# Low halves on VectorE alone, and the denominator's first step on ScalarE, in a top-k attention, expert and rational-layer kernel

## The chip, the cores and the metric

The kernel runs on one core of one Trainium2 chip. The metric is device microseconds (us) of one execution; the kernel before took 1326.49 us, the median of three runs (1324.46 to 1328.33). The engines are TensorE (PE in the profile, its weight loads PEld), VectorE (DVE), ScalarE (ACT), GpSimd (POOL) and SyncE (SP, which issues most DMAs).

## The reference, cut to what matters

```python
# 1. attention, 4 x 8 heads, 576 positions, head size 64, only the 32 largest scores of a row kept
# 2. routing: of all (token, expert) pairs, best first, each of 2304 tokens gets one of 8 experts,
#    each expert takes 288 tokens; then h = relu(x @ w1[e]) ; x2 = h @ w2[e]      (512 -> 1024 -> 512)
# 3. one more layer for all tokens, with a rational function in the middle:
h = x2 @ w_in                                    # 512 -> 2048
P = a[0] + a[1] * h + a[2] * h2 + a[3] * h3
Q = 1.0 + abs(b[0]) * abs(h) + abs(b[1]) * h2
out = (P / (Q + 1e-6)) @ w_out                   # 2048 -> 512
```

## The kernel before, in words

**Three stages.** First the attention, in 72 steps of 128 rows. Then the routing: seven phases, each of which finds by a search of four iterations the score down to which tokens are handed out (`route`, `search`, lines 1520 to 1735). An iteration is a chain: VectorE compares all tokens with 32 thresholds (L1502), TensorE counts (L1510), VectorE looks which thresholds are passed (L1574), TensorE spreads that (L1578), VectorE makes the next thresholds (L1586). At the end of a phase GpSimd marks the tokens handed out (L1665). Then the experts, one after the other, 288 tokens each: the first two products on `w1[e]` and `w2[e]` (the experts' own weights, made ready one expert ahead), and 16 units of the rational layer, each a slice of 128 of the 2048 columns.

**Matrices in two halves.** A float32 matrix is scaled by a power of two and stored as a high half and a low half in 16 bits; a product is then three 16-bit matmuls (`triple`, L1902 to L1904). ScalarE makes the high half (`high`, L437), and a second operation takes scaled value minus high half for the low one. `w_in` and `w_out` are cut in 32 pieces of 128 x 512, in four blocks of four each (`add_block`). A piece arrives by DMA, passes through some operations that rebuild its bits (`heads` on ScalarE, L374 to L386, and `mantissa`, `signed`, `apply_sign` on VectorE, L396 to L413), its sum of squares is taken (L307), the block gets its scale, and high and low halves follow. The high halves of a block wait for the low halves of the block before (L476), and the low half's end frees the raw piece's buffer; if a piece is still to come that may lie there, its DMA is issued then (`fetch`). Pieces 0 to 17 have buffers at the start; 18 to 23 wait for low halves; 24 to 31 lie where the first expert's raw weights were. The scales of all blocks of `w_out` together (`settle_out`) enter the rational layer's result, before its second product.

**A planner writes the order.** Each operation is a task with an engine, a cost, dependencies and a rank. `Flow.run` emits the task with the earliest start by its own reckoning, by rank where these tie; each engine then executes its instructions in the order written. During the search VectorE's tasks are emitted by `fill`, which is given a budget of 0.6 or 0.37 us at each place (J1, J2, J3 in L1529) and lets a VectorE task in only if its whole cost fits. Tasks of other engines only have to be able to start in time. After the search `flow.early` and, for the units, `flow.rest` emit all that is left. A low half is a VectorE task of cost 0.66 (L441) with an alternative: two GpSimd operations, cost 2.3, L449 and L450. The planner takes the alternative where GpSimd could start no later than 1 us after VectorE.

**A unit** (`add_unit`, from line 2151): TensorE makes `ph` (12 matmuls). ScalarE: z = |h| (L2169), uv = a3 h + a2 (L2172). VectorE: q = b1 z + b0 (L2175), q times z (L2178), uv times h (L2181), cube3 (L2193), which is the last to read `ph`. ScalarE: logarithm and exponential, for 1/Q (L2184, L2187). VectorE: two steps of correction (L2190, L2196) and the ratio (L2199). ScalarE and VectorE make its two halves (L1892, L1893), and TensorE adds 12 matmuls into `po`. `ph` has two buffers.

Of the kernel before, what the change touches and what calls it, by code (L numbers as in the profile page):

```python
# [8 lines left out]
F32 = mybir.dt.float32  # L9
# [5 lines left out]
AF = mybir.ActivationFunctionType  # L15
OP = mybir.AluOpType
# [168 lines left out]
def kernel(  # L185
# [15 lines left out]
    nc = tc.nc  # L201
# [5 lines left out]
    P = 128  # L207
# [40 lines left out]
    coef = consts.tile([P, 16], F32, name="coef")  # L248
# [81 lines left out]
    raw_t, todo = {}, list(range(NP - 8))  # L330

    flow = Flow()
# [3 lines left out]
    def fetch(slot, n=None):  # L336

        if n is None and todo and todo[0] <= slot[1]:
            n = todo.pop(0)
        if n is not None:  # L340
            nc.sync.dma_start(slot[0].bitcast(U16)[:, 0:2047], pieces[n][:, 1:2048])
            raw_t[n] = slot
            arrived[n].end = flow.transfer(1.5)
        elif slot[2] is not None:
            slot[2]()

    def value(n):
        return raw_t[n][0].rearrange("p (n w) -> p n w", w=2)[:, :, 1]
# [7 lines left out]
    def quick(n):  # L356
        return QS <= n < QE
# [36 lines left out]
    def signed(n, o):  # L394
        up = upper_of(n)[:, o]
        nc.vector.scalar_tensor_tensor(up, top_of(n)[:, o], 0x8000, up, op0=OP.bitwise_and, op1=OP.bitwise_or)  # L396

    def in_parts(cost, fn, deps, rank, late, hv=None):

        w = 512 // (hv or HV)  # L400
        return [
            flow.add("V", 0.06 + (cost - 0.06) * w / 512, lambda o=o: fn(slice(o, o + w)), deps, rank, late)
            for o in range(0, 512, w)
        ]
# [6 lines left out]
    def apply_sign(n, o=ALL):  # L411
        d = value(n).bitcast(F32)[:, o]
        nc.vector.tensor_tensor(d, d, sign(n)[:, o], op=OP.mult)  # L413
# [6 lines left out]
    def add_block(i, n0, dst, s, inv, rows, rank, late, after):  # L420

        o = slice(4 * i, 4 * i + 4) if rows else slice(i, i + 1)
        sq = wpool.tile([P, 4], F32, name="nq", bufs=8)
        steps = []
        n2 = sq
        if not rows:
            n2 = wpool.tile([P, 1], F32, name="nq1", bufs=8)
            steps.append(("V", 0.07, lambda: nc.vector.tensor_reduce(n2, sq, axis=AX.X, op=OP.add)))
        steps += [("V", 0.07, f) for f in power_steps(s[:, o], inv[:, o], n2, 410)]

        def part(g):
            j = 4 * i + g if rows else i
            return j, [d[:, j, :] if rows else d[:, i, g * 512 : (g + 1) * 512] for d in dst]

        def high(g):
            j, (h, l) = part(g)
            nc.scalar.activation(h, value(n0 + g).bitcast(F32), AF.Copy, scale=s[:, j : j + 1])  # L437

        def low(g):
            j, (h, l) = part(g)  # L440
            nc.vector.scalar_tensor_tensor(  # L441
                l, value(n0 + g).bitcast(F32), s[:, j : j + 1], h, op0=OP.mult, op1=OP.subtract
            )
            fetch(raw_t.pop(n0 + g))

        def low_pool(g):
            j, (h, l) = part(g)
            d = value(n0 + g).bitcast(F32)
            nc.gpsimd.tensor_tensor(d, d, s[:, j : j + 1].to_broadcast([P, 512]), op=OP.mult)  # L449
            nc.gpsimd.tensor_tensor(l, d, h, op=OP.subtract)  # L450
            fetch(raw_t.pop(n0 + g))

        norms = []
        for g in range(4):
            n = n0 + g
            t = [arrived[n]]
            if quick(n):
                first = flow.add("A", 0.52, lambda n=n: heads(n)[0][2](), t, rank + 0.5, late)
                t = flow.add("A", 0.52, lambda n=n: heads(n)[1][2](), [first], rank + 0.5, late)
                t = in_parts(0.6, lambda o, n=n: signed(n, o), [t], rank + 0.4, late)  # L460
                t = in_parts(0.6, lambda o, n=n: mantissa(n, o), t, rank + 0.3, late)
                take(first, ring_users, ZR, t)
            else:
                for k in range(3 if n >= 6 else 0):
                    t = [flow.add("A", (0.52, 0.52, 0.61)[k], lambda n=n, k=k: heads(n)[k][2](), t, rank + 0.5, late)]
                if n >= EV:
                    t = in_parts(0.6, lambda o, n=n: mantissa(n, o), t, rank + 0.4, late)
                    t = in_parts(0.6, lambda o, n=n: apply_sign(n, o), t, rank + 0.3, late)
            norms.append(
                flow.add("A", 0.61, lambda n=n, g=g: square(value(n).bitcast(F32), sq[:, g : g + 1]), t, rank + 0.2, late)  # L470
            )
        scaled = flow.chain(steps[:-1], norms, rank, late)
        lows, LOWS = [], after
        last = flow.chain(steps[-1:], [scaled], rank + 0.3, late)
        for g in range(4):
            t = flow.add("A", 0.61, lambda g=g: high(g), [scaled] + (lasts[-1] if lasts else []), rank + LOWS, late)  # L476
            t = flow.add("V", 0.66, lambda g=g: low(g), [t], rank + LOWS + 0.1, late)
            t.other = ("G", 2.3, lambda g=g: low_pool(g))
            lows.append(t)
        lasts.append(lows)  # L480
        return last
# [1383 lines left out]
    mp = ctx.enter_context(tc.tile_pool(name="mp", bufs=1, side="right"))  # L1865
# [8 lines left out]
    xe_t, tok_t, xT_t, hT_t, x2_t, sq_t, py_t, scl, bt = {}, {}, {}, {}, {}, {}, {}, {}, {}  # L1874
# [163 lines left out]
    def unscale(e):  # L2038
        inv2 = mp.tile([P, 1], F32, name="inv2", bufs=2)
        nc.vector.tensor_scalar(inv2, w_scale[1, e][1], w_scale[2, e][1], k_h, op0=OP.mult, op1=OP.mult)  # L2040
        inv2a = mp.tile([P, 1], F32, name="inv2a", bufs=2)
        nc.vector.tensor_scalar(inv2a, inv2, coef[:, 3:4], None, op0=OP.mult)
        back = mp.tile([P, 2], F32, name="back", bufs=2)
        nc.vector.tensor_scalar(
            back[:, 0:1].bitcast(I32), inv2.bitcast(I32), -1.0, float(254 << 23), op0=OP.mult, op1=OP.add
        )
        nc.vector.tensor_scalar(back[:, 1:2], back[:, 0:1], coef[:, 0:1], None, op0=OP.mult)
        scl[e] = [inv2, None, None, inv2a, back[:, 1:2]]

    def bound_steps(e):  # L2050
        st = {}
# [51 lines left out]
    for t in range(NT):  # L2103
        nc.gpsimd.memset(spacer, 0.0)
        s = nc.gpsimd.indirect_dma_start(
            out=order, out_offset=bass.IndirectOffsetOnAxis(ap=sloti[:, t : t + 1], axis=0),
            in_=row_id[:, t : t + 1], in_offset=None,
        )
# [42 lines left out]
    def add_unit(k):  # L2151

        e, f = divmod(k, NF2)
        st = {}
# [9 lines left out]
        def tile(name, n):  # L2164
            st[name] = tp.tile([P, CAP], F32, name=name, bufs=n)
            return st[name]
# [2 lines left out]
            nc.scalar.activation(tile("z", 3), st["ph"], AF.Abs, scale=scl[e][0])  # L2169

        def cube():
            nc.scalar.activation(tile("uv", 5), st["ph"], AF.Identity, scale=scl[e][3], bias=coef[:, 2:3])  # L2172

        def below():
            nc.vector.tensor_scalar(tile("qv", 4), st["z"], coef[:, 7:8], coef[:, 6:7], op0=OP.mult, op1=OP.add)  # L2175

        def below2():
            nc.vector.tensor_tensor(st["qv"], st["qv"], st["z"], op=OP.mult)  # L2178

        def cube2():  # L2180
            nc.vector.scalar_tensor_tensor(st["uv"], st["ph"], scl[e][0], st["uv"], op0=OP.mult, op1=OP.mult)  # L2181

        def log():
            nc.scalar.activation(tile("r", 4), st["qv"], AF.Ln, bias=coef[:, 14:15])  # L2184
# [29 lines left out]

        u = float(k)
        p = flow.add("P", 1.47, into, x2_of[e] + last["into"], u)
        a1 = flow.add("A", 0.39, size, [p, scales[e]], u)
        a3 = flow.add("A", 0.48, cube, [p, scales[e]], u)
        v1 = flow.add("V", 0.22, below, [a1], u + 0.05)
        g1 = flow.add("V", 0.34, below2, [v1], u + 0.05)  # L2220
        g2 = flow.add("V", 0.41, cube2, [a1, a3], u + 0.1)
        v3 = flow.add("V", 0.41, cube3, [g2], u + 0.1)
        a4 = flow.add("A", 0.38, log, [g1], u + 1.0)
        a5 = flow.add("A", 0.33, exp, [a4], u + 1.0)
        v2 = flow.add("V", 0.34, near, [a5], u + 1.2)
        v4 = flow.add("V", 0.34, nearer, [v2], u + 1.2)
        v5 = flow.add("V", 0.34, ratio, [v3, v4], u + 1.2)
        a6 = flow.add("A", 0.38, halves, [v5, bounds[e]], u + 2.0)
        v6 = flow.add("V", 0.37, lambda: st["steps"][1](), [a6], u + 2.1)
        p2 = flow.add("P", 1.47, out_of, [v6] + last["out"] + w_out_done[f // 4], u + OUT)  # L2230
        last.update(into=[p], out=[p2])
        hold(p, "ph", 2, [a1, a3, g2, v3])
# [67 lines left out]
    scales, bounds = {}, {}  # L2300
# [3 lines left out]
    for e in range(E):  # L2304
        u = 16.0 * e
        st = {}
        t = flow.add("P", 0.5, lambda e=e, st=st: st.update(pt=norm(e)), x2_of[e], u - 0.5)
# [13 lines left out]
        steps = add_steps(bound_steps(e), [v, scales[e], settled], u + 0.3)  # L2321
# [38 lines left out]
```

## Time and profile before

| what | value |
|---|---|
| median of three runs | 1326.49 us |
| the profiled execution | 1332.43 us, span 1330.7 us, 26771 instructions |
| PE busy | 1165.5 us, 88% of the span |
| DVE busy | 1214.8 us, 91% |
| ACT busy | 1060.3 us, 80% |
| POOL busy | 490.4 us, 37% |
| one expert, from 932.4 to 1009.8 us | 77.4 us |

Busy times are means over stages that differ: attention up to about 512 us, the search from there to about 620 us, the first expert's start until about 720 us, then the experts. What limits a stage is read from rows of that stage. Matmul ends are modelled in the profile, so that a busy TensorE need not be at its peak.

### The profile page before, as it was taken

How to read it: one execution, taken by the hardware profiler on the slowest of the kernel's cores; microseconds unless marked ns; L12 is line 12 of the kernel's file. 1: busy time of each engine (PE TensorE's matmuls, PEld its weight loads, DVE VectorE, ACT ScalarE, POOL GpSimd, SP SyncE). 2: the span in 40 equal slices, each digit the busy share in tenths (PEclk: the TensorE clock that was granted, in tenths of full speed). 3: DMA queues.
4: the chain of work that ended last, by engine and by line, in shares of the span. 5: the costliest groups of instructions: out<-in, count | busy, mean ns of one | idle time of the engine just before them, and what ended most of it. 6: DMA issues, size and time to landing. Idle time of an engine off the chain costs nothing.

```text
span 1330.7 us, 26771 instructions
## 1 busy us (share of the span) xinstructions
PE 1165.5 (88%) x9160; PEld 933.5 (70%) x9160; DVE 1214.8 (91%) x4672; ACT 1060.3 (80%) x2022; POOL 490.4 (37%) x500
## 2 busy tenths in 40 slices
PE   5899999999999896775566989999999999989995
PEld 4778888888888774443444767778777777867773
DVE  5999999999999966897689979999999999999994
ACT  5999999999999887587867877878878687866563
POOL 4878888877787800333722001010010101000010
PEclk9999999999999887555688999999999999999998
DMA  5204112021100304503232232112122211200000
GB/s 116 47 9 142 39 25 47 9 47 24 33 1 1 118 11 175 209 18 128 52 90 73 101 109 82 65 31 95 58 82 82 82 65 31 69 1 19 1 19 18
DMA packets 81732, 80.60 MB, mean 61 GB/s; under 512 B 60592, under 2 KB 60592, under 8 KB 81584
## 3 DMA queue, kind: packets, MB, share of 16 engines
q1 hardware_dynamic: 77888, 69.27, 16.8%
q0 software_dynamic: 3696, 9.50, 2.6%
q8 instruction: 76, 1.25, 0.4%
q14 instruction: 72, 0.59, 0.2%
HBM read 69.26 MB, written 9.48 MB: 59 GB/s over the span
## 4 chain that ended last, share of the span: by engine, by line
DVE 21%; issue 15%; PE 9%; ACT 4%; DMA 2%; POOL 1%; POOLq 0%
DVE uv L2199 2%; DVE uv L2181 2%; DVE qv L2178 2%; DVE g L1893 2%; DVE t L2196 2%; DVE t L2190 2%; DVE uv L2193 2%; DVE qv L2175 1%; ACT junk L307 1%; DVE w2s L1382 1%; PE pa L1902 1%; PE pa L1903 1%; PE pa L1904 1%; PE po L1903 1%; PE po L1902 1%
## 5 line engine op out<-in xcount | busy, mean ns | idle before, releaser
L768 POOL TENSOR_TENSOR win<-sv,sg 128x576 f32<-128x576 f32 x142 | 179.2, 1283 | 53.7 <-ACT sg L763 45.0
L742 DVE MAX8 cd<-sv 128x8 f32<-128x82 f32 (+1 forms) x1008 | 182.2, 228 | 17.8 <-ACT sv L696 17.8
L823 POOL TENSOR_TENSOR sv<-ex,sg 128x576 f32<-128x576 f32 x136 | 176.0, 1300 | 41.9 <-DVE sg L820 28.8
L1902 PE MATMUL ph<-x,win 128*128 128x288 f16 x512 | 147.5, 288 | 19.1 <-DVE uv L2193 18.8
L851 PEld LDWEIGHTS po<-vm,pT 128*128 128x128 f32 (+1 forms) x1280 | 145.6, 184 | 17.7 <-ACT pT L835 3.0
L851 PE MATMUL po<-vm,pT 128*128 128x65 f32 (+1 forms) x1280 | 152.3, 268 | 3.6 <-ACT pT L835 2.3
L1903 PE MATMUL po<-g,wout 128*128 128x288 f16 x512 | 147.2, 287 | 6.8 <-DVE g L1893 6.8
L1902 PE MATMUL po<-g,wout 128*128 128x288 f16 x512 | 147.4, 288 | 2.7 <-ACT g L1892 1.7
L2281 POOL DMA_INDIRECT out_dram<-ob,tok x24 | 26.1, 1089 | 331.0 <-ACT ob L2277 303.5
L1904 PE MATMUL ph<-x,win 128*128 128x288 f16 x512 | 147.7, 288 | 0.0
L1903 PE MATMUL ph<-x,win 128*128 128x288 f16 x512 | 147.6, 288 | 0.0
L1904 PE MATMUL po<-g,wout 128*128 128x288 f16 x512 | 147.2, 287 | 0.0
L1892 ACT ACTIVATE g<-uv,sgr 128x288 f16<-128x288 f32 x128 | 68.0, 532 | 71.6 <-DVE uv L2199 68.0
L1879 POOL DMA_INDIRECT xe<-xrows,rows_i x24 | 23.7, 986 | 261.8 <-PE pa L1914 170.5
L763 ACT ACTIVATE sg<-sv,cut_all 128x576 bf16<-128x576 f32 x142 | 109.2, 779 | 1.4 <-DVE cut_all L748 1.0
L829 PE MATMUL pt<-ident,sv 128*128 128x128 f32 x648 | 95.5, 286 | 11.4 <-POOL sv L823 9.2
L769 DVE MAX8 w<-win 128x8 f32<-128x576 f32 x142 | 105.0, 740 | 0.0
L817 ACT ACTIVATE ex<-sv,nb 128x576 f32<-128x576 f32 x136 | 104.1, 772 | 0.0
L2184 ACT ACTIVATE r<-qv,coef 128x288 f32<-128x288 f32 x128 | 68.0, 532 | 44.1 <-DVE qv L2178 43.3
L829 PEld LDWEIGHTS pt<-ident,sv 128*128 128x128 f32 x648 | 76.0, 146 | 37.0 <-POOL sv L823 22.3
L683 PE MATMUL s<-region 128*128 128x288 f32 (+5 forms) x400 | 92.7, 391 | 4.1 <-ACT sv L696 2.7
L696 ACT ACTIVATE sv<-s 128x576 f32<-128x576 f32 x144 | 85.3, 646 | 10.9 <-PE s L683 10.5
(372 smaller groups left out, 3581.6 us busy)
## 6 DMA issues: line engine op xcount, KB each, us to landing
region<-in_moe_w_dram SPq DMA_DIRECT2D x16, 2048.0 KB, 8.3
xrows<-x SPq DMA_DIRECT2D x1, 4644.0 KB, 21.9
region<-in_q_dram SPq DMA_DIRECT2D x32, 128.0 KB, 2.8
region<-in_k_dram SPq DMA_DIRECT2D x32, 128.0 KB, 2.9
vm<-in_v_dram SPq DMA_DIRECT2D x32, 128.0 KB, 3.1
wout<-in_moe_w_in_dram SPq DMA_DIRECT2D x8, 511.8 KB, 7.5
region<-in_moe_w_out_dram SPq DMA_DIRECT2D x8, 511.8 KB, 4.7
win<-in_moe_w_in_dram SPq DMA_DIRECT2D x6, 511.8 KB, 7.1
```

Source lines behind the costliest of these rows:

```text
L683: nc.tensor.matmul(ps[p0 : p0 + n, g, o : o + w], qT[:, hh, j, p0 : p0 + n], kT[:, bb, c : c + w], start=True, stop=True,)
L742: nc.vector.max(cd[:, g, :], sv[:, o : o + n])
L763: nc.scalar.activation(sg, sv_t[u, hh], AF.Sign, bias=cut_all[:, 2 * u + hh, 7:8], scale=-OVER, accum_out=t["sum"][:, c : c + 1],)
L768: nc.gpsimd.tensor_tensor(win, sv_t[u, hh], sg, op=OP.mult)
L769: later.append(lambda c=c, win=win: nc.vector.max(t["w8"][:, c, :], win))
L817: nc.scalar.activation(ex, sv, AF.Exp, bias=t["nb"][:, c : c + 1], scale=SCALE)
L823: nc.gpsimd.tensor_tensor(sv, ex, sg, op=OP.mult)
L829: nc.tensor.transpose(pt[:, c // 4, c % 4, :], pr[:, c * P : (c + 1) * P], ident)
L851: nc.tensor.matmul(po[p0 : p0 + n, i, hh, :], sb[:, hh * (R + 1) + c, p0 : p0 + n], vm[:, bb, hh, c, :], start=(c == 0), stop=False,)
L1902: nc.tensor.matmul(acc, ah, bh, start=first, stop=False)
L1903: nc.tensor.matmul(acc, ah, bl, start=False, stop=False)
L1904: nc.tensor.matmul(acc, al, bh, start=False, stop=last)
```

## The change

A low half has no alternative on GpSimd any more. In a unit, q = b1 z + b0 moves from VectorE to ScalarE; the scale of h is multiplied into the two factors of `cube` (two small operations per expert for one), so that `cube2` is a plain product of two tensors, without a per-partition factor. The planner gets other costs for all ScalarE and VectorE tasks of a unit.

```diff
-        def low_pool(g):
-            j, (h, l) = part(g)
-            d = value(n0 + g).bitcast(F32)
-            nc.gpsimd.tensor_tensor(d, d, s[:, j : j + 1].to_broadcast([P, 512]), op=OP.mult)
-            nc.gpsimd.tensor_tensor(l, d, h, op=OP.subtract)
-            fetch(raw_t.pop(n0 + g))
...
             t = flow.add("V", 0.66, lambda g=g: low(g), [t], rank + LOWS + 0.1, late)
-            t.other = ("G", 2.3, lambda g=g: low_pool(g))
...
-        nc.vector.tensor_scalar(inv2a, inv2, coef[:, 3:4], None, op0=OP.mult)
+        nc.vector.tensor_scalar(inv2a, inv2, coef[:, 3:4], inv2, op0=OP.mult, op1=OP.mult)
+        inv2b = mp.tile([P, 1], F32, name="inv2b", bufs=2)
+        nc.vector.tensor_scalar(inv2b, inv2, coef[:, 2:3], None, op0=OP.mult)
...
-            nc.scalar.activation(tile("uv", 5), st["ph"], AF.Identity, scale=scl[e][3], bias=coef[:, 2:3])
+            nc.scalar.activation(tile("uv", 5), st["ph"], AF.Identity, scale=scl[e][3], bias=scl[e][5])
...
-            nc.vector.tensor_scalar(tile("qv", 4), st["z"], coef[:, 7:8], coef[:, 6:7], op0=OP.mult, op1=OP.add)
+            nc.scalar.activation(tile("qv", 4), st["z"], AF.Identity, scale=coef[:, 7:8], bias=coef[:, 6:7])
...
-            nc.vector.scalar_tensor_tensor(st["uv"], st["ph"], scl[e][0], st["uv"], op0=OP.mult, op1=OP.mult)
+            nc.vector.tensor_tensor(st["uv"], st["ph"], st["uv"], op=OP.mult)
...
-        a1 = flow.add("A", 0.39, size, [p, scales[e]], u)
-        a3 = flow.add("A", 0.48, cube, [p, scales[e]], u)
-        v1 = flow.add("V", 0.22, below, [a1], u + 0.05)
-        g1 = flow.add("V", 0.34, below2, [v1], u + 0.05)
+        a1 = flow.add("A", 0.43, size, [p, scales[e]], u)
+        a3 = flow.add("A", 0.5, cube, [p, scales[e]], u)
+        v1 = flow.add("A", 0.5, below, [a1], u + 0.05)
+        g1 = flow.add("V", 0.43, below2, [v1], u + 0.05)
...
```

The other costs of a unit go from 0.33 to 0.41 up to 0.38 to 0.48 in the same way.

## Rows read from the trace of the kernel before

**Rows 1.** Windows by stage: busy us (count) of PE, PEld, DVE, ACT, POOL; clock; DMA.
```profile
631.50:706.00 74.50, 45.62 (x276) 31.95 (x277) 55.91 (x171) 54.30 (x109) 33.22 (x46) 0.76 0.28 68
705.00:720.00 15.00, 4.80 (x33) 3.44 (x33) 14.86 (x44) 10.57 (x23) 6.90 (x6) 0.83 0.01 1
720.00:785.00 65.00, 60.63 (x483) 47.20 (x482) 61.45 (x151) 55.06 (x105) 0.00 (x0) 0.99 0.36 130
785.00:932.40 147.40, 140.72 (x1142) 111.33 (x1140) 141.00 (x371) 113.73 (x232) 13.83 (x18) 1.00 0.21 68
932.40:1009.80 77.40, 74.97 (x610) 59.35 (x609) 76.25 (x200) 60.06 (x124) 6.43 (x9) 1.00 0.21 71
1164.60:1310.00 145.40, 134.67 (x1081) 105.49 (x1080) 139.91 (x358) 93.83 (x200) 6.81 (x12) 1.00 0.03 9
```
**Rows 2.** GpSimd's timeline in the search: start, us, operation, idle before it.
```profile
526.28 0.43 POOL L1665 TENSOR_TENSOR asg<-oh,gone 128x144 bf16<-128x144 bf16 x1 [9.31 <-DVE gone L1659]
539.25 0.43 POOL L1665 TENSOR_TENSOR asel<-oh,gone 128x144 bf16<-128x144 bf16 x1 [12.54 <-DVE gone L1659]
...
542.90 1.04 POOL L449 TENSOR_TENSOR win<-win,s_in 128x512 f32<-128x512 f32 x1 [2.68 <-ACT win L437]
544.02 1.25 POOL L450 TENSOR_TENSOR win<-win 128x512 f16<-128x512 f32 x1
...
616.25 0.44 POOL L1665 TENSOR_TENSOR asel<-oh,gone 128x144 bf16<-128x144 bf16 x1 [5.46 <-DVE gone L1659]
```
**Rows 3.** GpSimd's groups, 540 to 700 us: count, busy us, mean ns, idle.
```profile
L449 POOL TENSOR_TENSOR wout<-wout,s_in 128x512 f32<-128x512 f32 x6 | 7.1, 1188 | 3.9 <-ACT win L437 3.9
L449 POOL TENSOR_TENSOR win<-win,s_in 128x512 f32<-128x512 f32 x6 | 7.0, 1174 | 5.4 <-ACT win L437 5.4
```
**Rows 4.** VectorE's groups, 512 to 542 us.
```profile
L1502 DVE TENSOR_TENSOR cmp<-vt,thr 128x288 bf16<-128x288 f32 x18 | 7.4, 453 | 0.2
L1586 DVE SCALAR_TENSOR_TENSOR thr<-step,pt,nxt 128x32 f32<-128x32 f32 x6 | 1.5, 253 | 0.6 <-PE pt L1578 0.5
```
**Rows 5.** The same groups, 542 to 623 us.
```profile
L1502 DVE TENSOR_TENSOR cmp<-vt,thr 128x288 bf16<-128x288 f32 x38 | 23.8, 667 | 0.5
L1586 DVE SCALAR_TENSOR_TENSOR thr<-step,pt,nxt 128x32 f32<-128x32 f32 x15 | 6.3, 419 | 0.0
```
**Rows 6.** VectorE's timeline: a wait in the search, then its first low half, and later.
```profile
537.51 0.16 DVE L428 TENSOR_REDUCE nq<-nq 128x1 f32<-128x4 f32 x1 [1.59 <-ACT junk L307]
...
644.15 0.75 DVE L441 SCALAR_TENSOR_TENSOR win<-wout,s_in,win 128x512 f16<-128x512 f32 x1
...
682.43 0.17 DVE L1911 CAST tok<-xe 96x3 int32<-96x3 f32 x1 [5.51 <-DMA xe<-xrows,rows_i]
...
687.51 2.73 DVE L441 SCALAR_TENSOR_TENSOR wout<-region,s_out,wout 128x512 f16<-128x512 f32 x4
```
**Rows 7.** ScalarE's groups on the pieces, 540 to 720 us.
```profile
L437 ACT ACTIVATE win<-wout,s_in 128x512 f16<-128x512 f32 x8 | 5.8, 745 | 1.0 <-DVE s_in L296 1.0
...
L384 ACT ACTIVATE wout<-wout 128x512 int8<-128x512 bf16 x4 | 5.4, 1357 | 5.8 <-DMA wout<-in_moe_w_out_dram 5.8
L385 ACT ACTIVATE wout<-wout 128x512 bf16<-128x512 bf16 x4 | 5.4, 1342 | 0.1
```
**Rows 8.** A unit's groups over the whole span.
```profile
L2172 ACT ACTIVATE uv<-ph,coef,inv2a 128x288 f32<-128x288 f32 x128 | 74.7, 584 | 0.5 <-DVE g L1893 0.5
...
L2184 ACT ACTIVATE r<-qv,coef 128x288 f32<-128x288 f32 x128 | 68.0, 532 | 44.1 <-DVE qv L2178 43.3
...
L2181 DVE SCALAR_TENSOR_TENSOR uv<-ph,inv,uv 128x288 f32<-128x288 f32 x128 | 65.2, 509 | 0.0
...
L2178 DVE TENSOR_TENSOR qv<-qv,z 128x288 f32<-128x288 f32 x128 | 57.9, 452 | 1.3
L2187 ACT ACTIVATE r<-r 128x288 f32<-128x288 f32 x128 | 56.2, 439 | 2.2
L2175 DVE TENSOR_SCALAR qv<-z,coef 128x288 f32<-128x288 f32 x128 | 54.2, 423 | 2.4 <-ACT z L2169 2.2
```

More of the change, by code (lines that the diff above doesn't have):

```diff
@@ L2047, in unscale @@
         nc.vector.tensor_scalar(back[:, 1:2], back[:, 0:1], coef[:, 0:1], None, op0=OP.mult)
-        scl[e] = [inv2, None, None, inv2a, back[:, 1:2]]
+        scl[e] = [inv2, None, None, inv2a, back[:, 1:2], inv2b]
     def bound_steps(e):
@@ L2216, in add_unit @@
         p = flow.add("P", 1.47, into, x2_of[e] + last["into"], u)
-        a1 = flow.add("A", 0.39, size, [p, scales[e]], u)
-        a3 = flow.add("A", 0.48, cube, [p, scales[e]], u)
-        v1 = flow.add("V", 0.22, below, [a1], u + 0.05)
-        g1 = flow.add("V", 0.34, below2, [v1], u + 0.05)
[L2221 to L2229, printed above, removed]
+        a1 = flow.add("A", 0.43, size, [p, scales[e]], u)
+        a3 = flow.add("A", 0.5, cube, [p, scales[e]], u)
+        v1 = flow.add("A", 0.5, below, [a1], u + 0.05)
+        g1 = flow.add("V", 0.43, below2, [v1], u + 0.05)
+        g2 = flow.add("V", 0.44, cube2, [a1, a3], u + 0.1)
+        v3 = flow.add("V", 0.48, cube3, [g2], u + 0.1)
+        a4 = flow.add("A", 0.46, log, [g1], u + 1.0)
+        a5 = flow.add("A", 0.38, exp, [a4], u + 1.0)
+        v2 = flow.add("V", 0.43, near, [a5], u + 1.2)
+        v4 = flow.add("V", 0.43, nearer, [v2], u + 1.2)
+        v5 = flow.add("V", 0.48, ratio, [v3, v4], u + 1.2)
+        a6 = flow.add("A", 0.46, halves, [v5, bounds[e]], u + 2.0)
+        v6 = flow.add("V", 0.48, lambda: st["steps"][1](), [a6], u + 2.1)
         p2 = flow.add("P", 1.47, out_of, [v6] + last["out"] + w_out_done[f // 4], u + OUT)
```

## Prediction

> **What bounds the kernel now.** I read the page's summary first, then windows by stage, then for each stage the groups by line, the waits and the timelines. The page alone misleads: VectorE's 91% and TensorE's 88% are means over stages with different limits. Three stages are touched by the change.
>
> In the experts [rows 1] one expert takes 77.4 us, in which VectorE is busy 76.25, TensorE 74.97 and ScalarE 60.06. VectorE is the fullest, but TensorE is only 1.3 us behind it; the reader is to see that a lighter VectorE can give back at most TensorE's idle 2.43 us per expert. From 1164.6 to 1310, where no weights are split any more, TensorE idles 145.4 - 134.67 = 10.7 us and VectorE 5.5.
>
> In the search (about 512 to 620 us) the chain VectorE, TensorE, VectorE sets the pace, and GpSimd disturbs it. GpSimd marks the end of each phase at L1665. From 526.28 to 539.25, with no low half on GpSimd, a phase takes 12.97 us; the five from 539.25 to 616.25 take 77.0 / 5 = 15.40 [rows 2]. GpSimd's low halves begin at 542.90, twelve of them up to the search's end, each of two operations of some 1.2 us [rows 2, 3]. The same compare of 128x288 takes 453 ns before 542 us and 667 after, the new thresholds 253 and 419 ns [rows 4, 5].
>
> Between search and units [rows 1], 631.5 to 706, no engine is full (VectorE 55.9 of 74.5 us, ScalarE 54.3, TensorE 45.6 at a clock of 0.76): a chain of pieces, transfers and the first expert's layers. Then, from 705 to 720, TensorE has 4.8 us of work in 15 and VectorE is full (14.86): the units wait for the scales of w_out.
>
> **The change part by part.** I add it up against the profiled execution, 1332.4 us, which lies 5.9 us above the median shown.
>
> *Search: GpSimd's low halves go.* 24 GpSimd operations vanish. If the five phases fall to the one undisturbed phase, 5 x (15.40 - 12.97) = 12.2 us are saved. The excess of the two groups alone is 38 x 0.214 + 15 x 0.166 = 10.6 us [rows 4, 5], which fits. The undisturbed phase itself holds a wait of 1.59 us for ScalarE [rows 6]; without it, it would be 11.38 and the saving 20. The other end is 0: VectorE's stalls could be replaced by its waits for TensorE's counts, which also splits the first expert's weights in the search. I take -12, because both ways of counting come near it.
>
> The Trainium skill, page "SBUF — State Buffer", section "Who interferes with whom", says that a VectorE instruction with two SBUF inputs and a GpSimd instruction that reads SBUF exclude each other for a whole instruction. By that rule alone all of GpSimd's time on the low halves could be VectorE's stall, 12 x 2.4 = 29 us [rows 2, 3], and the total 17 us lower than mine; the phases bear out 12 of it, since not each GpSimd operation meets such an instruction of the chain.
>
> *After the search: the twelve low halves come back.* The planner can't put them into the search: a low half costs 0.66 and no budget there is over 0.6. The trace agrees: VectorE's first low half starts at 644.15, after the search [rows 6]. So twelve low halves, at 2.73 / 4 = 0.68 us each [rows 6], 8.2 us, move behind the search on VectorE. Since the high halves of a block wait for the low halves of the block before, eight high halves move with them (8 x 0.75 = 6.0 us on ScalarE [rows 7]), and so do the DMA issues of pieces 18 to 21, on SP's queue, which these low halves released. Queued behind a piece that has not arrived are, in ScalarE's order, the first expert's own evacuations: today ScalarE loses 5.8 us to one such wait [rows 7]. Cover: VectorE idles 18.6 and ScalarE 20.2 us from 631.5 to 706 [rows 1]. Lower end: 0, all in that cover. Upper end: all of it in a row, 8.2 + 6.0 + one more wait of 5.8 + the two long conversions of four pieces, 4 x 2.7 = 10.8 [rows 7], together 31 us. I take +8: VectorE's part in full, because from 682.4 on VectorE hardly pauses and the scales of w_out stand at the end of exactly that work; ScalarE's part stays in its idle time. The three remaining low halves of GpSimd lie between 705 and 720 (6 operations, [rows 1]) and cost 3 x 0.68 = 2.0 us of a full VectorE there; the first units, five by then, give back 5 x 0.48 (below), so I set both at nothing; without that return they cost 2.0.
>
> *Units: one operation from VectorE to ScalarE.* VectorE loses L2175, 423 ns, and L2181 falls from 509 to about the 452 of L2178, which multiplies two tensors without a factor [rows 8]: 0.48 us per unit, 7.7 per expert, so 68.6 instead of 76.25. ScalarE's new operation has two per-partition operands. The row without one is 439 ns, with one 532, so 93 each and 625 with two; from `ph` the two-operand form takes 584 [rows 8]. ScalarE gets 16 x 0.625 = 10.0 us per expert, 70.1 of at most 77.4. TensorE, 74.97, is then the fullest. The chain of one unit gets longer by about 0.2 us, hidden by the next unit's matmuls; without that cover it costs 0.2 x 128 = 26 us. Two small operations per expert become three, 8 x 0.2 = 2 us over the kernel at most, beside other work. What is late next is TensorE itself, and ScalarE where weights are prepared.
>
> How much of TensorE's idle time comes back? From 720 to 785 nothing: ScalarE is busy 55.06 of 65 [rows 1] and gets 13 units x 0.625 = 8.1 more, so it is full there. Elsewhere the idle time is 6.7 (785 to 932.4), 3 x 2.43 (the expert shown and two that follow alike) and 10.7 (1164.6 to 1310), in all 24.7 us [rows 1]. I take half, -12: TensorE's waits there end at VectorE's results, which now come earlier, but in-order queues with ScalarE at 90% will leave some. Ends: -25, and +26 if ScalarE's longer operation is paid in each unit.
>
> *The planner's costs* rise towards the measured durations and change the order in the units. I can't work out that order; I set it at nothing, between the ends just given.
>
> Sum: -12 + 8 - 12 = -16: 1316 us in a profile, and 1326.5 - 16 = 1310 for a timed run.
>
> **The rivals.** *The moved work decides (slower).* If low halves, high halves, transfer and conversions after the search run one after the other, the scales of w_out come 31 us late and TensorE waits: -12 + 31 - 12 = +7, 1333 us. For it: TensorE already idles there for these scales, and ScalarE executes in order. Against it: the 18.6 and 20.2 us of idle time. It turns the sign once the delay is over 24 us.
>
> *ScalarE takes VectorE's place.* The units gain nothing, -12 + 8 + 0 = -4, 1322 us. For it: from 720 to 785 ScalarE would be full. Against it: 70 of 77 us in an expert.
>
> *Each unit pays the dearer operation.* 0.2 us in each of 128 units, -12 + 8 + 26 = +22, 1348 us. Against it: ScalarE waited 43.3 us in all for the product before the logarithm [rows 8], so that it has room. The Trainium skill, page "ScalarE: Activation LUTs", section "Rules for kernel authors", speaks for this rival: it says to use VectorE rather than ScalarE for additions and multiplications. The trace agrees on the price (423 against about 625 ns [rows 8]) but shows VectorE as the fuller engine, so I give it little.
>
> *All comes back.* The search saves 20, the delay after it is 5, the experts gain 22: -37, 1289 us. For it: the undisturbed phase still held a wait, and the planner's costs come nearer to the chip's.
>
> *The change doesn't do what it says:* if low halves did run within the search, their 8.2 us would lie there instead, and the sum is the same; the profile would tell it, not the time.
>
> **How the numbers follow.** Forecast 0.55, its own range 1301 to 1319; the moved work decides 0.10; ScalarE takes VectorE's place 0.15; each unit pays 0.05; all comes back 0.15. A change of under 0.3%, 4 us, can't be told from none. Faster (under 1322.5): 0.55 + 0.15 + half of 0.15 = 0.78; the same: 0.10; slower: 0.12. The range, 1290 to 1327, leaves out the lower half of the last case and the two slow ones, some 0.2.
>
> **What would show it.** In the profile after: no L449 or L450 group; compares in the search at about 0.45 us throughout and phases of 12.5 to 13.5 us between the markings. VectorE has all 32 low halves, none before the search's end, and the conversions of pieces 18 to 23 lie later against the search's end than now. The stretch of idle TensorE before the first `po` products starting about as long as now. One expert at 75.5 to 76.5 us with TensorE at 98%, VectorE near 69 and ScalarE near 70. I am wrong if the phases stay above 15 us, if the first `po` products come later than at 725 us, or if an expert still takes 77.4 us.

## The result, and the profile after

The changed kernel takes 1297.17 us, median of four runs (1295.58 to 1299.1), against 1327.41 of the kernel before: a ratio of 0.9774, 95% interval 0.975 to 0.980. That is 30 us less where 16 were forecast; the direction and the range of 1290 to 1327 held, but the forecast's own range, 1301 to 1319, was missed by 4 us. The profiled execution took 1299.1 us, its span is 1297.4.

Line numbers after the change are 8 lower than before up to the unit's helpers and 6 lower in the unit (L1502 is now L1494, L2181 is L2175). I cut both spans, to 0.1 us, at the same three events: GpSimd's first marking of the search, the copy of `x_max` on VectorE that closes the search's stage, and the first `g` on VectorE (the first unit is nearly done). The stage from `x_max` to the first `g` is called the delay below.

| from ... to | before | after | change | forecast |
|---|---|---|---|---|
| start to the first marking (not touched) | 526.3 | 526.9 | +0.6 | 0 |
| first marking to `x_max` | 107.2 | 90.9 | -16.3 | -12 |
| `x_max` to the first `g` | 85.0 | 94.5 | +9.5 | +8 |
| first `g` to the end | 612.2 | 585.1 | -27.1 | -12 |
| span | 1330.7 | 1297.4 | -33.3 | -16 |

The page's first line, after:

```profile
PE 1154.9 (89%) x9160; PEld 932.5 (72%) x9160; DVE 1150.7 (89%) x4567; ACT 1115.1 (86%) x2150; POOL 458.6 (35%) x470
```

VectorE is busy 64 us less and ScalarE 55 us more than before; where the time went is again to be read by stage.

*The search.* GpSimd's timeline after, answering to [rows 2], and VectorE's groups from 526.9 to 601.4 us, answering to [rows 4, 5]:

```profile
526.91 0.43 POOL L1657 TENSOR_TENSOR asg<-oh,gone 128x144 bf16<-128x144 bf16 x1 [9.30 <-DVE gone L1651]
539.90 0.43 POOL L1657 TENSOR_TENSOR asel<-oh,gone 128x144 bf16<-128x144 bf16 x1 [12.56 <-DVE gone L1651]
...
552.04 0.43 POOL L1657 TENSOR_TENSOR asel<-oh,gone 128x144 bf16<-128x144 bf16 x1 [11.17 <-DVE rng L1530]
...
601.42 0.49 POOL L1657 TENSOR_TENSOR asel<-oh,gone 128x144 bf16<-128x144 bf16 x1 [11.16 <-DVE gone L1651]
```

```profile
L1494 DVE TENSOR_TENSOR cmp<-vt,thr 128x288 bf16<-128x288 f32 x48 | 19.8, 452 | 0.6
...
L1578 DVE SCALAR_TENSOR_TENSOR thr<-step,pt,nxt 128x32 f32<-128x32 f32 x18 | 4.5, 248 | 0.0
```

No low half is left on GpSimd, and the compare and the threshold keep 452 and 248 ns throughout, where before they went to 667 and 419. The five phases from 539.90 to 601.42 take 12.30 us each, against 15.40.

*The experts.* Windows of the changed kernel (columns as in [rows 1]), two single experts:

```profile
912.90:986.70 73.80, 73.80 (x613) 59.66 (x612) 67.93 (x180) 66.16 (x141) 7.31 (x9) 1.00 0.19 67
986.70:1060.33 73.63, 73.63 (x610) 59.49 (x609) 71.02 (x187) 67.65 (x143) 5.99 (x9) 1.00 0.30 102
```

An expert takes 73.6 to 73.8 us instead of 77.4, and TensorE is busy in all of it; VectorE and ScalarE both have some us left. Not every expert is alike, so here are six together, from the second expert's first `g` to the eighth's, before and after:

```profile
805.05:1264.37 459.32, 442.11 (x3583) 349.80 (x3582) 449.48 (x1165) 341.44 (x708) 33.73 (x48) 1.00 0.17 55
```

```profile
800.01:1235.20 435.19, 433.16 (x3567) 349.04 (x3566) 405.87 (x1069) 380.66 (x800) 34.21 (x46) 1.00 0.17 58
```

That is 76.6 us each before and 72.5 after. The unit's operations (ScalarE from 800 to 1290 us, VectorE from 712), answering to [rows 8]:

```profile
L2169 ACT ACTIVATE qv<-z,coef 128x288 f32<-128x288 f32 x109 | 68.7, 631 | 0.0
L2166 ACT ACTIVATE uv<-ph,inv2b,inv2a 128x288 f32<-128x288 f32 x108 | 63.9, 592 | 0.0
```

```profile
L2175 DVE TENSOR_TENSOR uv<-ph,uv 128x288 f32<-128x288 f32 x123 | 55.4, 450 | 7.4 <-ACT uv L2166 6.7
```

The new operation costs 631 ns (625 forecast), the plain product 450 (452 forecast).

*Between search and units.* What the changed kernel waits for, from its timelines of GpSimd, TensorE, VectorE and SP's queue, and two of its windows:

```profile
664.10 1.24 POOL L2106 DMA_DIRECT2D rows_i<-order  x1 [13.25 <-DMA order<-row_id,sloti]
...
672.00 0.42 PE L1906 MATMUL pa<-ident,xe 96*128 96x96 f32 x1 [14.31 <-DMA xe<-xrows,rows_i]
...
674.39 0.17 DVE L1903 CAST tok<-xe 96x3 int32<-96x3 f32 x1 [12.56 <-DMA xe<-xrows,rows_i]
...
633.99 6.62 SPq L341 DMA_DIRECT2D wout<-in_moe_w_out_dram  x6
```

```profile
640.00:650.00 10.00, 6.34 (x50) 4.67 (x48) 4.98 (x12) 4.50 (x8) 8.23 (x17) 1.00 1.05 205
...
660.00:670.00 10.00, 0.00 (x0) 0.00 (x0) 1.43 (x5) 6.17 (x12) 2.21 (x2) 0.56 0.04 1
```

The wait for the scatters in the kernel before:

```profile
671.80 1.24 POOL L2112 DMA_DIRECT2D rows_i<-order  x1 [4.86 <-DMA order<-row_id,sloti]
```

The reader is to see that the lost time is idle time. After the search GpSimd scatters the tokens' numbers (`order`), reads them back (`rows_i`) and gathers the second expert's rows (`xe`); `tok` on VectorE is the first there to read them. Before, `rows_i` waited 4.86 us for the last scatter and VectorE 5.51 for the gather [rows 6]; now it is 13.25 and 12.56, and from 660 to 670 TensorE does nothing and VectorE 1.4 us of work. Six pieces of `w_out` go out in one burst at 634, and the DMA engines are full from 640 to 650. Cut at `tok`, the delay before is 48.9 and 36.0 us, and after it is 56.6 and 38.0: 7.7 of the 9.5 us lie before the gathered rows are there, 2.0 behind.

### The profile page after: what moved, and what is told of

It reads as the page before. It is cut to its first block, busy times and chain, and to the rows that moved or that the text cites. A ratio compares the mean times of both kernels' runs of the same rounds, so it can differ in the third digit from the quotient of the medians.

```text
span 1297.4 us, 26750 instructions
## 1 busy us (share of the span) xinstructions
PE 1154.9 (89%) x9160; PEld 932.5 (72%) x9160; DVE 1150.7 (89%) x4567; ACT 1115.1 (86%) x2150; POOL 458.6 (35%) x470
## 4 chain that ended last, share of the span: by engine, by line
PE 23%; issue 15%; ACT 5%; DVE 4%; POOL 3%; DMA 2%; POOLq 0%; DVEq 0%
PE pa L1894 3%; PE pa L1896 3%; PE pa L1895 3%; PE po L1895 2%; PE po L1896 2%; PE po L1894 2%; PE ph L1894 2%; PE ph L1896 2%; PE ph L1895 2%; POOL order L2099 2%; ACT junk L307 1%; DMA order<-row_id,sloti 1%; POOL out_dram L2275 1%; DMA region<-in_moe_w_dram 1%; DVE wout L441 1%
## 5 line engine op out<-in xcount | busy, mean ns | idle before, releaser
L688 ACT ACTIVATE sv<-s 128x576 f32<-128x576 f32 x144 | 85.4, 647 | 11.2 <-PE s L675 10.9
L2163 ACT ACTIVATE z<-ph,inv 128x288 f32<-128x288 f32 x128 | 64.1, 501 | 35.2 <-PE ph L1896 32.3
L675 PE MATMUL s<-kT,region 128*128 128x288 f32 (+5 forms) x400 | 90.0, 378 | 2.1 <-ACT sv L688 2.0
```

The source lines that it names most:

```text
L675: nc.tensor.matmul(ps[p0 : p0 + n, g, o : o + w], qT[:, hh, j, p0 : p0 + n], kT[:, bb, c : c + w], start=True, stop=True,)
```

## The experiments

Theories at the start: for the delay after the search T1 (the burst of transfers holds up scatters and gather) and T2 (the prediction's: VectorE's low halves lie on the path); for the experts U1 (VectorE's lighter load lets TensorE run full) and the rival that the planner's new costs do it. All stage lengths are from one profile each; ratios are to the kernel before on the same chip, with 95% intervals.

| kernel | first marking to `x_max` | `x_max` to first `g` | first `g` to end | ratio |
|---|---|---|---|---|
| before | 107.2 | 85.0 | 612.2 | 1 |
| lows_only | 90.1 | 91.5 | 618.7 | 1.002 [1.000, 1.004] |
| units_only | 106.3 | 84.6 | 585.9 | 0.980 [0.976, 0.984] |
| before_new_costs | 106.2 | 84.4 | 604.8 | 0.997 [0.994, 0.999] |
| after_old_costs | 90.8 | 92.7 | 593.7 | 0.981 [0.977, 0.985] |
| changed kernel, again | 90.0 | 94.1 | 585.1 | 0.976 [0.974, 0.979] |
| short_pieces | 90.1 | 90.7 | 584.9 | 0.974 [0.971, 0.977] |
| double_lows | 90.3 | 95.2 | 586.1 | 0.975 [0.972, 0.977] |
| lighter | 90.0 | 89.8 | 582.0 | 0.973 [0.970, 0.976] |
| pool_reads | 106.8 | 91.8 | 585.9 | 0.986 [0.983, 0.988] |
| pool_writes | 91.0 | 86.8 | 585.8 | one run, 1291.34 us |
| lows_early | 93.0 | 95.2 | 587.5 | 0.981 [0.978, 0.984] |
| gather_36 | 90.0 | 89.2 | 583.1 | 0.968 [0.966, 0.970] |

**lows_only: the low halves alone.** The kernel before, with

```diff
-        def low_pool(g): ...
-            t.other = ("G", 2.3, lambda g=g: low_pool(g))
```

> The kernel before, with GpSimd's way of making low halves taken out, and nothing else of the change. If the change's parts add up by stage as its trace suggests: the five phases of the search fall from 77.0 to about 61.5 us (-15.5), the delay from the search's end to the first expert's g on VectorE rises from 85.0 to about 94 us (+8 to +9.5), the experts keep 77.4 us each, so about -5 to -8 us against the kernel before (1319 to 1322). Rival, that the planner's new costs and the lighter units shorten the search as well: phases well above 12.5 us here. Rival, that the delay comes from the units: it stays near 85 us here, and the kernel is 15 us faster.

The search fell as expected, the delay rose as expected, and yet the kernel is not faster: ratio 1.002. The stage after the first `g`, expected unchanged, took 6.5 us more. Windows from `x_max` to the first `g` and from there to the end, of the kernel before and of this one:

```profile
633.50:718.50 85.00, 48.45 (x300) 34.02 (x301) 68.27 (x205) 61.25 (x124) 38.78 (x51) 0.78 0.25 59
718.50:1330.70 612.20, 569.39 (x4566) 447.17 (x4565) 576.51 (x1488) 446.78 (x917) 43.08 (x63) 0.99 0.18 58
```

```profile
617.80:709.30 91.50, 53.93 (x300) 35.04 (x301) 73.19 (x216) 68.57 (x133) 36.46 (x46) 0.73 0.31 78
709.30:1328.00 618.70, 569.30 (x4566) 447.13 (x4565) 578.07 (x1491) 448.52 (x918) 42.91 (x63) 0.99 0.17 58
```

13 of the 17 us won in the search are given back; over the timed runs nothing is left. From `x_max` to the end VectorE is busy 651.3 us instead of 644.8, since GpSimd's share is its own now, and idle 58.9 instead of 52.4. What is lost behind the first `g` is lost before the second expert's first `g`: from there to the eighth's, both kernels take 459.3 us. That first stretch, in the kernel before and in this one, and 20 us out of it:

```profile
718.45:805.05 86.60, 79.30 (x625) 61.43 (x625) 78.25 (x209) 71.24 (x137) 2.88 (x4) 0.98 0.30 105
```

```profile
709.31:803.99 94.68, 80.88 (x625) 62.19 (x625) 79.78 (x212) 73.21 (x138) 2.81 (x4) 0.96 0.27 96
...
770.00:790.00 20.00, 16.62 (x116) 12.55 (x116) 8.03 (x19) 10.71 (x22) 2.81 (x4) 0.84 0.39 135
```

It is 8.1 us longer (the kernel's end takes 1.6 less), with 1.5 us more of VectorE's work; VectorE idles from 770 to 790 above all. So half of the 13 us is VectorE's added work, and half is waiting whose cause no run shows.

**units_only: the rest of the change.** The changed kernel, with the same lines put back.

> The changed kernel, with GpSimd's way of making low halves put back: the units' edit and the planner's costs alone. If the parts add up: phases of 15.4 us as before, a delay of about 85 us, experts of 73.7 us, so the experts' part of the gain alone, some -25 to -30 us (1298 to 1303), about as fast as the whole change. Rival, that the experts gain only because the first expert's start came otherwise (low halves no longer on GpSimd between 705 and 720 us): an expert above 75 us and less than -15 us.

As expected: the search and the delay stay as before, the experts gain their 26.3 us. So the units' part alone gives nearly all of the gain, and the low halves' part, worth nothing on the kernel before, adds little to it (0.980 against 0.976 to 0.977, with intervals that overlap). With the lighter units it is paid for in the delay alone (94.5 against 84.6 us): from the first `g` on, the changed kernel and this one take 585.1 and 585.9 us. Why nothing is lost behind the first `g` then, no run shows.

**before_new_costs and after_old_costs: load or order?**

```diff
 # before_new_costs: the kernel before, unit tasks at the new costs (v1 stays on VectorE, 0.41)
-        a1 = flow.add("A", 0.39, size, [p, scales[e]], u)
+        a1 = flow.add("A", 0.43, size, [p, scales[e]], u)
...
 # after_old_costs: the changed kernel, unit tasks at the old costs (v1 on ScalarE, 0.5)
-        a1 = flow.add("A", 0.43, size, [p, scales[e]], u)
+        a1 = flow.add("A", 0.39, size, [p, scales[e]], u)
```

> The kernel before with the change's planner costs in the units and no other edit (the multiply-and-add stays on VectorE, at 0.41). Theory that VectorE's load decides in the experts (76.25 of 77.4 us): an expert stays at 77 us or above, within 5 us of before. Rival, that the order found with costs nearer to the measured durations decides: an expert at 74 to 75.5 us, 10 to 20 us faster than before.

> The changed kernel with the planner's old costs in the units (ScalarE's new operation keeps 0.5, since it has no old cost). Theory that the lighter VectorE decides: an expert at 73.6 to 74.2 us, within 5 us of the changed kernel. Rival, that the order by the new costs decides: an expert back at 75.5 to 77 us, 12 to 25 us slower than the changed kernel.

Both count. Without the new costs the lighter VectorE takes the stage after the first `g` from 612.2 to 593.7 us (-18.5); the costs take another 8.6 (593.7 to 585.1), and 7.4 on the kernel before. Six experts from the second on take 74.0 us each with the lighter VectorE at the old costs and 72.5 at the new; on the kernel before, 76.6 and 76.1. By the ratios the costs are worth 0.3 to 0.5%, and for the changed kernel the intervals overlap. So the rival's 10 to 25 us was off in both runs, and the theory's "within 5" about right, though the stage alone shows 7 to 9 us.

**lighter: is TensorE the limit now?** The changed kernel without the last step of the reciprocal:

```diff
         def near():
-            nc.vector.scalar_tensor_tensor(tile("t", 2), st["qv"], 1.0 + 1e-6, st["r"], op0=OP.add, op1=OP.mult)
+            pass
...
         def nearer():
-            nc.vector.scalar_tensor_tensor(st["t"], st["t"], 2.0, st["r"], op0=OP.subtract, op1=OP.mult)
+            pass
...
-            nc.vector.scalar_tensor_tensor(st["uv"], st["uv"], scl[e][4], st["t"], op0=OP.add, op1=OP.mult)
+            nc.vector.scalar_tensor_tensor(st["uv"], st["uv"], scl[e][4], st["r"], op0=OP.add, op1=OP.mult)
```

> The changed kernel without the last step of the reciprocal in each unit (the two VectorE operations near and nearer are left out, the ratio takes the exponential's result): VectorE's load falls by some 0.8 us per unit, 13 us per expert. Theory U1, TensorE is full in the changed kernel (73.63 of 73.63 us): an expert stays at 73.4 to 73.8 us, and the whole gains under 5 us, from the stage between 705 and 785 us alone. Rival U2, VectorE's chain still sets the pace and TensorE's records only look full: an expert falls to 71 to 72.5 us, the whole by over 10 us.

Windows of two of its experts:

```profile
855.30:929.10 73.80, 73.80 (x612) 59.48 (x610) 60.13 (x156) 68.59 (x146) 5.80 (x9) 1.00 0.22 75
986.00:1059.60 73.60, 73.60 (x610) 59.47 (x609) 60.53 (x153) 67.39 (x143) 5.82 (x9) 1.00 0.29 100
```

VectorE has 60 instead of 68 to 71 us of work and the expert still takes 73.6 to 73.8: TensorE is the limit of the changed kernel's experts (counted from start to start it hardly waits either, see below). The 4 us that this kernel gains are not an expert's: its delay is 4.7 us shorter, and the intervals of the two ratios overlap.

**double_lows: T2 by itself.** The changed kernel, the twelve low halves that came to VectorE written twice:

```diff
+            if not rows and i < 3:
+                nc.vector.scalar_tensor_tensor(
+                    l, value(n0 + g).bitcast(F32), s[:, j : j + 1], h, op0=OP.mult, op1=OP.subtract
+                )
```

> The changed kernel in which each of the twelve low halves of w_in that came to VectorE is written twice, 12 x 0.68 = 8.2 us more of VectorE's work right after the search and nothing else. T2, VectorE's low halves are on the path: the delay from the search's end to the first g rises from 94.5 to about 102 us, the kernel by 6 to 8 us. T1, the transfers are: the delay rises by 0 to 3 us, since VectorE waits there anyway.

```profile
617.85:713.10 95.25, 51.70 (x298) 35.06 (x299) 79.00 (x222) 67.84 (x132) 30.99 (x46) 0.73 0.38 75
```

VectorE is busy 79.0 us in the delay, against 69.9 in the changed kernel, and the delay is 0.7 to 1.1 us longer. The low halves of `w_in` lie where VectorE waits anyway: T2 falls.

**short_pieces: T1 by itself.** The changed kernel, with

```diff
+            if 18 <= n < 24:
+                nc.sync.dma_start(slot[0].bitcast(U16)[:, 0:31], pieces[n][:, 1:32])
+            else:
                 nc.sync.dma_start(slot[0].bitcast(U16)[:, 0:2047], pieces[n][:, 1:2048])
...
```

The constants that stand in for the missing columns are left out here.

> The changed kernel in which the transfers of w_out's pieces 18 to 23 bring 16 of 1024 columns; the rest of these pieces isn't loaded and constants take the place of their exponents. Every instruction keeps its size and place. Theory T1: the longer delay between the search's end and the first g (94.5 us against 85.0) comes from these six transfers, issued in one burst, which hold up GpSimd's scatters of order, the gather of the second expert's rows and the pieces themselves. Then the delay falls to 84 to 88 us, the wait for order from 13.25 to under 6 us, and the kernel is 6 to 10 us faster than the changed one (about 1288 to 1292). Theory T2, of the prediction: VectorE's twelve low halves make it. Then the delay stays at 92 to 95 us and the time within 3 us of the changed kernel.

```profile
664.88 1.24 POOL L2114 DMA_DIRECT2D rows_i<-order  x1 [7.12 <-DMA order<-row_id,sloti]
```

The wait for `order` fell to 7.12 us, but the delay only to 90.7, and the ratio's interval overlaps the changed kernel's. Kernels with the full burst had that wait at 7.37 (lows_only) and 7.81 us (lighter) as well. So the burst may hold the scatters up by some us, but it isn't shown to be most of what the delay gained: neither theory explains it.

**pool_reads and pool_writes: what slowed the search.** The changed kernel with dummy operations on GpSimd, on a tile of their own, in every second phase:

```diff
+        def noise(g):
+            for _ in range(2):
+                nc.gpsimd.tensor_tensor(pool_d, pool_d, pool_d, op=OP.mult)   # pool_writes: memset(pool_d, 1.0)
+        for g in range(4 if not rows else 0):
+            flow.add("G", 2.3, lambda g=g: noise(g), [scaled], rank + LOWS, late)
...
```

> The changed kernel with two dummy products of 128x512 floats on GpSimd, on a tile of their own, where it had made each of the twelve low halves. Theory: the search was slow since GpSimd's operations stretch VectorE's: phases that meet such operations rise from 12.3 to 14 us or above, the compares from 0.41 toward 0.6 us or more. Rival: the search was slow through something else that went with the low halves (the transfers that they released, their rows of the order): phases stay at 12.3 us.

> The changed kernel with GpSimd's dummy products in the search replaced by as many memsets of 128x512 floats, which write and read nothing. If GpSimd's reads stretch VectorE's operations, the phases that took 18.0 us beside the products fall back to 12.0 to 12.6 us; if any access of GpSimd does it, they stay at 15 us or above.

GpSimd's timeline in both, and VectorE's groups in the phase beside the dummy operations:

```profile
537.65 0.43 POOL L1665 TENSOR_TENSOR asel<-oh,gone 128x144 bf16<-128x144 bf16 x1 [11.74 <-DVE gone L1659]
...
538.57 9.98 POOL L469 TENSOR_TENSOR poold<-poold 128x512 f32<-128x512 f32 x8
555.61 0.43 POOL L1665 TENSOR_TENSOR asel<-oh,gone 128x144 bf16<-128x144 bf16 x1 [7.06 <-DVE rng L1538]
...
567.61 0.43 POOL L1665 TENSOR_TENSOR asel<-oh,gone 128x144 bf16<-128x144 bf16 x1 [11.04 <-DVE rng L1538]
```

```profile
L1502 DVE TENSOR_TENSOR cmp<-vt,thr 128x288 bf16<-128x288 f32 x8 | 5.0, 663 | 0.1
...
L1586 DVE SCALAR_TENSOR_TENSOR thr<-step,pt,nxt 128x32 f32<-128x32 f32 x3 | 1.5, 506 | 0.0
...
L1564 DVE TENSOR_TENSOR low<-thr,step 128x1 f32<-128x1 f32 x4 | 1.4, 361 | 0.0
```

```profile
538.20 0.43 POOL L1665 TENSOR_TENSOR asel<-oh,gone 128x144 bf16<-128x144 bf16 x1 [11.75 <-DVE gone L1659]
...
539.10 4.60 POOL L469 MEMSET poold<- 128x512 f32 x8
550.73 0.43 POOL L1665 TENSOR_TENSOR asel<-oh,gone 128x144 bf16<-128x144 bf16 x1 [7.04 <-DVE rng L1538]
```

```profile
L1502 DVE TENSOR_TENSOR cmp<-vt,thr 128x288 bf16<-128x288 f32 x8 | 3.3, 452 | 0.1
...
L1586 DVE SCALAR_TENSOR_TENSOR thr<-step,pt,nxt 128x32 f32<-128x32 f32 x3 | 0.7, 249 | 0.0
```

Beside eight products a phase takes 17.96 us, beside eight memsets 12.53; the same phase of the changed kernel takes 12.14 (539.90 to 552.04). All 24 products together bring the stage from the first marking to `x_max` back to 106.8 us, the 107.2 of the kernel before. The products' data have nothing to do with the search, so GpSimd's products themselves are shown to be what stretched it, and its writes are not; what a product does beyond a memset is to read and to multiply. The memsets are shorter (4.60 us against 9.98), but per us of GpSimd's time, too, they cost 0.08 us against 0.58. The Trainium skill, page "SBUF — State Buffer", section "Who interferes with whom", says that a VectorE instruction with two SBUF inputs contends with a GpSimd instruction that reads SBUF and not with one that only writes it. These runs agree: 5.8 us more against 0.4. They also measure what the prediction left between 12 and 29 us: eight products of 9.98 us cost 5.8, some 60% of GpSimd's time.

The surprise is in the delay: 86.8 us beside the memsets, 8 less than in the changed kernel. From `tok` to the first `g` 29.3 us pass in both dummy kernels, against 38.0. The planner had given each dummy group 2.3 us of GpSimd's time, so it may have taken the gather to come later and put other work ahead of it. That is theory T3: conversions and low halves of `w_out` stand behind the gather in the engines' orders, and the engines wait for it with work in hand.

**lows_early: can T3 be had by earlier low halves?**

```diff
...
-            t = flow.add("V", 0.66, lambda g=g: low(g), [t], rank + LOWS + 0.1, late)
-            lows.append(t)
+            lows += in_parts(0.66, lambda o, g=g: low(g, o), [t], rank + LOWS + 0.1, late)
...
-        ins = [add_block(c, 4 * c, w_in_s, s_in, i_in, False, c - 80.0, False, 20.0) for c in range(KC)]
+        ins = [add_block(c, 4 * c, w_in_s, s_in, i_in, False, c - 80.0, False, 1.0) for c in range(KC)]
```

> The changed kernel whose low halves are made by VectorE in two parts of 256 columns (0.36 each to the planner) and stand early in the order for w_in, so that the planner puts them into the search's gaps; the transfers that they release go out one after the other in the search. Theory T3: the delay after the search is longer in the changed kernel (94.5 us against 85.0) since the pieces 18 to 23 come later, and their conversions and seven low halves of w_out then stand behind the gather of the second expert in the engines' orders. Then the delay falls to 84 to 88 us, phases stay at 12.2 to 13 us, and the kernel is 4 to 9 us faster than the changed one. Rival: VectorE has no gaps in the search; twelve low halves, 8 to 10 us, lengthen the five phases to 13.5 to 14.3 us, and the total stays within 3 us of the changed kernel.

> The changed kernel itself, on the same chip as the variant with early low halves, to compare with: a ratio to the kernel before of 0.975 to 0.980.

A miss. Eight of the twelve low halves ran in the search, which grew by 2 to 3 us, and the delay stayed at 95.2: the last pieces' transfers still went out together after the search (six, issued from 625.45 us on), and their conversions stayed behind the gather. At 0.981 it is no gain over the changed kernel on the same chip (0.976; the intervals just touch).

**gather_36: the order alone.**

```diff
-    flow.free["G"] = max(flow.free["G"], flow.free["V"]) + 24.0
+    flow.free["G"] = max(flow.free["G"], flow.free["V"]) + 36.0
```

> The changed kernel in which the planner takes GpSimd to be busy with the scatters of order for 36 us instead of 24 after the search, so that it puts the conversions of w_out's pieces ahead of the work that needs the second expert's gathered rows; no instruction is added, removed or resized. Theory T3, the order: the changed kernel's longer delay (94.5 us) comes from conversions and low halves that stand behind the gather in the in-order engines, while these wait for it. Then the time between the landing of the gather and the first g falls from 38 to about 29 us as beside the memsets, the delay to 85 to 89 us, the kernel to about 1288 to 1293 (ratio 0.968 to 0.972). Rival, that the memsets' kernel was faster by chance of a single run, or for its GpSimd work: a ratio of 0.974 to 0.980 like the changed kernel's.

Its windows beside those of the changed kernel above, and from `x_max` on, with the changed kernel's after it:

```profile
660.00:670.00 10.00, 0.39 (x4) 0.08 (x1) 9.43 (x28) 10.00 (x20) 3.05 (x2) 0.65 0.03 1
...
615.10:704.30 89.20, 48.08 (x297) 33.40 (x298) 70.59 (x210) 67.74 (x131) 41.23 (x46) 0.71 0.42 89
704.30:1287.40 583.10, 560.00 (x4570) 447.59 (x4568) 527.67 (x1377) 501.12 (x1048) 43.00 (x63) 0.99 0.18 60
```

```profile
617.80:712.30 94.50, 50.81 (x298) 34.93 (x299) 69.87 (x209) 67.50 (x131) 35.63 (x46) 0.73 0.33 75
712.30:1297.40 585.10, 558.51 (x4568) 446.92 (x4567) 528.76 (x1378) 502.68 (x1048) 44.35 (x63) 0.99 0.18 61
```

Nothing is computed otherwise, and the delay falls by 5.3 us: VectorE's work in it is the same (70.6 against 69.9 us), its idle time falls from 24.6 to 18.6. TensorE still waits 13.4 us for the gather, and `tok` even comes later (62 us after `x_max` instead of 57), but from 660 to 670 VectorE and ScalarE now convert pieces, and 27 us instead of 38 pass between `tok` and the first `g`. The kernel takes 1289.89 us (1288.74 to 1292.81), ratio 0.968 [0.966, 0.970]: better than both kernels. So the order is shown to be worth 5 us of delay. It is not shown to be what the change had lengthened: the kernel before has 36.0 us from `tok` to the first `g`, nearly as many as the changed kernel's 38.0. Whether the same edit would speed up the kernel before was not run.

## Why the prediction was right in sign and off in size

**"A lighter VectorE can give back at most TensorE's idle 2.43 us per expert"** is the step that failed. An expert gave back 3.6 to 3.8 us. TensorE's busy time is not its floor: a matmul of the unit is recorded with 0.29 us, but the next one starts 0.12 us later, as in these two lines of the changed kernel:

```profile
713.94 0.29 PE L1894 MATMUL po<-g,wout 128*128 128x288 f16 x1
714.06 0.29 PE L1895 MATMUL po<-g,wout 128*128 128x288 f16 x1
```

So the recorded end covers up to 0.17 us of waiting behind each matmul. It shows in the sums: from the first `g` to the end TensorE makes 4566 and 4568 recorded matmuls, in 569.4 us of busy time before and 558.5 after, at a granted clock of 0.99 in both. Of the 27.1 us that this stage gained, 16.2 were idle time in the profile before and 10.9 stood there as busy. Counted from start to start instead, with all beyond 0.125 us as waiting, TensorE waits 46.6 us in this stage before and 20.0 after: 26.6 of the 27.1 us. In the expert of [rows 1] it waits 3.6 us by this count, not 2.43, and in each of the two experts shown after, 0.01.

**"I take half, -12"** failed with it: the term should have been -27, just beyond its end of -25. In the six experts of the windows above, TensorE's waits by the same count are 23.1 us before, 10.2 in after_old_costs and 2.1 in the changed kernel (1.2 in lighter). About half comes back by the moved operation and the lighter product alone, nearly all with the new costs.

**"I set it at nothing"**, said of the planner's costs, failed as well: they are worth 8.6 us of that stage (after_old_costs), 7.4 on the kernel before.

**The search** was mis-sized, not misread: -16.3 instead of -12. The only undisturbed phase to be seen took 12.97 us and held a wait of 1.59 for ScalarE, which the prediction had named; without GpSimd's reads the phases take 12.0 to 13.1.

**After the search**, +8 was nearly the measured +9.5, for the wrong reason. "VectorE's part in full" doesn't hold: 8 us more of the same work cost about 1 us (double_lows). VectorE's busy time in the delay rose by 1.6 us and its idle time by 7.9 (16.7 to 24.6). gather_36 wins 5.3 us by another order, but behind `tok`, where the change had added only 2.0 of its 9.5 us. The other 7.7 are open: `tok` came 48.9 us after `x_max` in the kernel before, and 50.6 to 56.6 in lows_only, after_old_costs, lighter and the changed kernel, which all have the same burst of transfers, so that short_pieces (52.8) doesn't tell.

**The sum** took the stages as independent. They aren't: alone, the low halves' part is worth nothing (lows_only), since 6.5 us come on top in the delay and 6.5 behind it, all before the second expert; with the lighter units nothing is lost behind the first `g`. The prediction weighed that price for the delay and set it at nothing in the units.

**What held.** From the first `g` to the second expert's first `g` nothing came back (86.6 us before, 87.7 after), as forecast; ScalarE is the fullest engine there after the change, busy 81.0 us, but that this is the reason was not tested. The prices of the unit's operations were right within 6 ns. The Trainium skill, page "ScalarE: Activation LUTs", section "Rules for kernel authors", would have left the multiply-and-add on VectorE; the runs agree with it on the price (631 against 423 ns [rows 8]) and show the opposite choice, together with the lighter product and the costs, to be worth 2% (units_only), in experts where VectorE was the fullest engine; the move alone was not run. The rival "ScalarE takes VectorE's place" came true in that stretch alone, "each unit pays the dearer operation" nowhere, and "all comes back" is nearest for the experts (22 us, measured 27), but not for the search (20, measured 16) or the delay (5, measured 9.5).

## What to carry to other kernels

A TensorE that looks 97% busy may have 5% to give, because recorded matmul ends hide short waits: count its floor from the distance of starts in an undisturbed run. When work moves from a helper engine to a chain engine, measure *each later stage* as well: here 13 of 17 us came back as a loss, half of them as waits. When two in-order engines stand idle at a late transfer, look at what is queued behind it before blaming the transfer: one number in the planner won 5 us here, though the transfer came no earlier.

## What the runs showed of the hardware

GpSimd's products of 128x512 stretched even VectorE's smallest operations: the 128x1 subtraction `low` took 361 ns in the phase beside them (above) and 153 in the next phase of pool_reads, from 555.61 to 567.61 us:

```profile
L1564 DVE TENSOR_TENSOR low<-thr,step 128x1 f32<-128x1 f32 x4 | 0.6, 153 | 0.0
```

Memsets of the same size, 0.57 us each, left compare and threshold at 452 and 249 ns.
